# Filler matmuls between the last expert and the output: ten of 64 columns instead of four of 256

## The chip, the core and the metric

One core of one Trainium2 chip runs the whole kernel as one program. The metric is the device time of that core in microseconds (us). Single instructions are given in us or ns. The engines are called PE (TensorE, matrix multiply; PEld is its weight load), DVE (VectorE), ACT (ScalarE), POOL (GpSimd) and SP (SyncE, which here only issues DMAs).

## What is computed

A gated recurrence over 5056 tokens of 4 sequences, 256 channels, is followed by a soft mixture of experts. All tokens are mixed into 32 slots (a softmax over tokens), each of 8 experts transforms its own 4 slots, and each token of the output is a softmax-weighted mixture of the 32 slot outputs:

```python
for t in range(S):                      # S = 5056
    h = f[:, t] * h + i[:, t] * x[:, t]
    y[:, t] = h
# y is then reshaped to 20224 tokens of 256 and called x
logits = x @ phi                        # 20224 x 32
slot_input = softmax(logits, axis=0).T @ x
for e in range(E):                      # E = 8, w1: 256 x 1024, w2: 1024 x 256
    h = np.maximum(slot_input[e] @ w1[e], 0.0)
    slot_out[e] = h @ w2[e]
return softmax(logits, axis=1) @ slot_out.reshape(32, 256)   # 20224 x 256, float32
```

## The kernel before, in words

The kernel has three stages. **The recurrence stage** (lines 452 to 579, about the first 131 us) loads x and f_logit in groups, applies the gates, turns the data to channels on PE, scans along time on DVE, turns it back, and builds the exponentials of the logits, `etall`, and the 32 slot inputs. All instructions stand in an order written out by hand (`manual_schedule`, line 151), so every engine works through its own list in the order of the code.

**The expert stage** (lines 583 to 686, about 131 to 145.5 us) is short and runs on PE almost alone. The second half of the experts is accumulated into two PSUM tiles `so_ps`, one for each half of the 256 output columns (lines 661 to 668). Then DVE scales the first half and ACT the second half into the SBUF tile `slot_out` (lines 683 and 684), and POOL makes from it the two masked copies `slot_bd` (line 686).

**The output stage** (lines 689 to 795) multiplies `etall` with `slot_out` (`share`, line 704) or with `slot_bd` (`couple`, line 753) on PE into the PSUM tiles `op`, scales the rows with `rrow` on DVE (lines 694 and 758) and ACT (lines 698 and 764) into SBUF, and sends the rows out by DMAs that SP issues (lines 730, 741, 767 and 784). The order is that of lines 787 to 795: first block 0 of sequence 0 in small pieces (`pieces`), so that the first DMAs can go out early, then larger parts.

What the change touches is the helper `spin` (lines 143 to 146). It multiplies a piece of the first expert's weights with itself into the PSUM tile `tail`, whose values nobody reads: it is filler, and keeps PE occupied where PE would otherwise wait. Each of its matmuls loads 128 columns of weights and then streams `w` columns. It is called in four places between the slots and the output, in two of them with 21 matmuls of 64 columns, in one with 7 of 256 columns (`SPINS`), and at line 682, after the last expert matmul and before the first output matmul, with 4 of 256 columns (`D` is 256, `P` is 128).

The order around the change is this: on PE the last `so_ps` matmul, the filler of line 682, the first output matmul of line 704; on DVE and ACT the `slot_out` halves, then the first evictions of `op`. The PSUM of the output tiles `op` is the memory that `tail` and the other PSUM tiles leave behind (`held.close()`, line 689), so the first output matmul waits for three things: the DVE half of `slot_out`, the ACT half, and the end of PE's own filler.

Of the kernel before, what the change touches and what calls it, by code (L numbers as in the profile page):

```python
# [18 lines left out]
def kernel(  # L19
# [11 lines left out]
    B, S, D = x.shape  # L31
# [4 lines left out]
    P = 128  # L36
# [106 lines left out]
    def spin(dst, k, w):  # L143
        for _ in range(k):
            nc.tensor.matmul(dst[:, ds(0, w)], w1_sb[0][:, 0, :P], w1_sb[0][:, 0, :w],  # L145
                             start=True, stop=True, skip_group_check=True)
# [9 lines left out]
    with tc.tile_pool(name="sp2", bufs=3) as sp2, \  # L156
# [314 lines left out]
        for n in range(n_unit):  # L471
# [14 lines left out]
            else:  # L486
# [40 lines left out]
                if n == n_unit - 2:  # L527
                    tail = psp.tile([P, 2, G], F32, name="tail", tag="sp")
# [61 lines left out]
    with tc.tile_pool(name="ew", bufs=1) as ew, \  # L590
# [70 lines left out]
        for j in range(Q):  # L661
# [13 lines left out]
            if j == 1:  # L675
# [3 lines left out]
                spin(tail[:, 1], SPINS, D)  # L679
                nc.vector.reciprocal(rrow[:, wide_r:q], rs_ps[:, wide_r:q])  # L680
                nc.vector.reciprocal(rrow[:, q, ds(0, B // 2)], rs_ps[:, q, ds(0, B // 2)])
        spin(tail[:, 1], 4, D)
        nc.vector.tensor_scalar_mul(slot_out[:, ds(0, C)], so_ps[0], rcs)
        nc.scalar.activation(slot_out[:, ds(C, C)], so_ps[1], ACT.Copy, scale=rcs)
        for u in range(2):
# [140 lines left out]
```

## Time and profile before

| | |
|---|---|
| median of 4 runs | 200.76 us (200.65 to 200.94) |
| the profiled execution's own time | 200.85 us |
| its span, first to last instruction | 199.1 us |
| mean granted TensorE clock | 0.861 |
| PE / PEld / DVE / ACT / POOL busy | 152.9 / 110.1 / 143.4 / 138.6 / 103.0 us |
| HBM read, written | 58.23 MB, 20.71 MB |

The profile is one execution; its span is 1.75 us shorter than its time. Times of single instructions are counted from the start of the span. "Granted clock" is the share of its full clock that PE was given. "Busy" of PE is not PE at its peak, since matmuls overlap and their ends are modelled. A releaser is the instruction whose end the profile sees as the last thing that an instruction waited for.

### The profile page before, as it was taken

The page shows a single profiled execution, that of the slowest core. Times are in us where ns is not written, and L with a number is a line of the kernel's source. Part 1 is how long each engine was busy: PE and PEld are TensorE (multiplying, and loading weights), DVE is VectorE, ACT ScalarE, POOL GpSimd, SP SyncE. Part 2 cuts the span into 40 slices and gives each one's busy share as a digit, 9 for nine tenths or more (in the row PEclk, how much of TensorE's full clock was granted, in tenths as well). Part 3 has the DMA queues.
Part 4 walks back from the last instruction along what each step waited for, and adds up shares of the span by engine and source line. Part 5 has one row for each costly group of instructions (what it writes and reads, how often), then busy time and mean ns, then how long its engine had stood idle before and what let it go on. Part 6 is the DMA issues. An engine that isn't in the chain of part 4 may idle for free.

```text
span 199.1 us, 3497 instructions
## 1 busy us (share of the span) xinstructions
PE 152.9 (77%) x1330; PEld 110.1 (55%) x1330; DVE 143.4 (72%) x164; ACT 138.6 (70%) x195; POOL 103.0 (52%) x78
## 2 busy tenths in 40 slices
PE   0588598898979989899897987989989999950000
PEld 0367467676757767668585765567963543310000
DVE  1669879999787999999989999614268878740000
ACT  3689678799688998999987595623069889980000
POOL 2489587884986789774969969390030000000000
PEclk9999979999987999999999999999996555555555
DMA  5999999999999999999999999999429999999995
GB/s 180 414 421 421 433 421 421 433 428 343 391 425 423 426 323 418 426 413 321 397 421 391 220 213 212 211 218 207 79 90 426 419 441 421 421 454 438 421 421 214
DMA packets 14449, 70.77 MB, mean 355 GB/s; under 512 B 1745, under 2 KB 3025, under 8 KB 10465
## 3 DMA queue, kind: packets, MB, share of 16 engines
q1 hardware_dynamic: 11664, 62.13, 75.4%
q0 software_dynamic: 2624, 8.42, 21.2%
q8 instruction: 10, 0.16, 0.3%
q14 instruction: 7, 0.05, 0.1%
q10 hardware_dynamic: 144, 0.00, 0.0%
HBM read 58.23 MB, written 20.71 MB: 397 GB/s over the span
## 4 chain that ended last, share of the span: by engine, by line
PE 41%; DVE 24%; DMA 8%; ACT 8%; issue 4%; POOL 4%; SPq 0%; ACTq 0%; DVEq 0%; POOLq 0%
DVE h L304 17%; PE op L753 12%; DMA f_t<-in_f_logit_dram 8%; PE hp L317 4%; POOL u_t L237 4%; PE up L258 4%; PE sp L252 4%; DVE ht L334 4%; ACT s_t L226 3%; PE op L704 2%; PE slot_ps L174 2%; PE so_ps L664 2%; PE lg L348 2%; ACT a L293 2%; PE tail L145 1%
## 5 line engine op out<-in xcount | busy, mean ns | idle before, releaser
L237 POOL TENSOR_TENSOR u_t<-s_t,x_t 128x1024 bf16<-128x1024 bf16 (+1 forms) x39 | 82.6, 2130 | 24.4 <-ACT s_t L226 11.3
L304 DVE TENSOR_TENSOR_SCAN h<-a,h,up 128x512 bf16<-128x512 f32 (+1 forms) x72 | 86.9, 1252 | 5.5 <-PE up L258 3.8
L226 ACT ACTIVATE s_t<-f_t 128x2048 bf16<-128x2048 f32 (+2 forms) x23 | 38.3, 1670 | 6.4 <-DMA f_t<-in_f_logit_dram 6.3
L317 PE MATMUL hp<-ident_f,h 128*128 128x128 f32 (+1 forms) x160 | 29.6, 310 | 8.3 <-DVE ht L334 5.5
L317 PEld LDWEIGHTS hp<-ident_f,h 128*128 128x128 f32 (+1 forms) x160 | 23.2, 208 | 16.4 <-DVE ht L334 9.7
L252 PE MATMUL sp<-ident_f,s_t 128*128 128x128 f32 x144 | 22.0, 298 | 9.7 <-ACT s_t L226 7.7
L286 ACT ACTIVATE a<-sp,nomlb 128x1024 f32<-128x1024 bf16 x24 | 25.4, 1113 | 1.6 <-PE sp L252 1.0
L753 PE MATMUL op<-slot_bd,etall 64*128 64x512 bf16 x62 | 24.3, 592 | 0.3
L252 PEld LDWEIGHTS sp<-ident_f,s_t 128*128 128x128 f32 x144 | 17.9, 154 | 11.4 <-issue 5.9
L764 ACT ACTIVATE oc<-op,rrow 128x256 f32<-128x256 f32 x60 | 22.8, 490 | 1.4 <-PE op L753 0.9
L758 DVE TENSOR_TENSOR oc<-op,rrow 128x1024 f32<-128x1024 f32 x16 | 19.2, 1222 | 4.7 <-PE op L753 4.6
L293 ACT ACTIVATE a<-sp,nomlb 128x512 f32<-128x512 bf16 (+2 forms) x22 | 17.9, 859 | 4.3 <-PE sp L252 3.9
L258 PE MATMUL up<-ident_f,u_t 64*128 64x64 f32 x192 | 18.2, 233 | 2.6 <-POOL u_t L237 2.5
L258 PEld LDWEIGHTS up<-ident_f,u_t 64*128 64x128 f32 x192 | 14.3, 141 | 6.6 <-POOL u_t L237 3.2
L174 PE MATMUL slot_ps<-rep,ident 128*128 128x256 bf16 x122 | 17.6, 280 | 0.0
L753 PEld LDWEIGHTS <-etall 64*128 64x128 bf16 x62 | 9.0, 152 | 14.2 <-issue 11.8
L334 ACT COPY ht<-hp 128x512 f32<-128x512 f32 (+1 forms) x18 | 10.5, 582 | 8.3 <-PE hp L317 8.3
L334 DVE COPY ht<-hp 128x512 f32<-128x512 f32 (+1 forms) x22 | 14.7, 668 | 1.1 <-PE hp L317 1.1
L174 PEld LDWEIGHTS <-ident 128*128 128x128 bf16 x126 | 11.3, 101 | 3.1 <-issue 1.1
L304 DVE TENSOR_TENSOR_SCAN h<-a,up 128x512 bf16<-128x512 f32 x8 | 9.4, 1212 | 2.7 <-ACT a L293 1.9
L252 PE MATMUL up<-ident_f,u_t 128*128 128x128 f32 x48 | 9.7, 334 | 0.8 <-POOL u_t L237 0.8
L348 PE MATMUL lg<-h,phi 128*32 128x512 bf16 (+1 forms) x80 | 10.1, 412 | 0.0
(105 smaller groups left out, 147.2 us busy)
## 6 DMA issues: line engine op xcount, KB each, us to landing
f_t<-in_f_logit_dram SPq DMA_DIRECT2D x12, 1024.0 KB, 12.7
x_t<-in_x_dram SPq DMA_DIRECT2D x12, 1024.0 KB, 11.5
out_dram<-oc SPq DMA_DIRECT2D x6, 2048.0 KB, 13.4
w_sb<-in_moe_w_dram POOLq DMA_DIRECT2D x14, 512.0 KB, 9.5
f_t<-in_f_logit_dram SPq DMA_DIRECT2D x12, 512.0 KB, 8.7
x_t<-in_x_dram SPq DMA_DIRECT2D x12, 512.0 KB, 8.6
out_dram<-oc SPq DMA_DIRECT2D x4, 896.0 KB, 6.0
out_dram<-ob SPq DMA_DIRECT2D x1, 2048.0 KB, 9.1
```

What stands on the lines that cost most here:

```text
L174: nc.tensor.matmul(slot_bank[:, 1, ds(0, rhs.shape[1])], ident, rhs, start=first and i < 2, stop=False, skip_group_check=True)
L226: nc.scalar.activation(s_t, f_t, ACT.Sigmoid, scale=-1.0)
L237: nc.gpsimd.tensor_tensor(uts[n][:, :r], s_t[:, :r], x_t[:, :r], ALU.mult)
L252: nc.tensor.transpose(ps[:, :, r], t[:, r], ident_f)
L258: nc.tensor.transpose(v[:, :, r], t(r)[k].bitcast(F32), ident_f[k, k])
L286: nc.scalar.activation(a, sp[:, :, :, :, o], ACT.Identity, scale=nomlb[:, ds(o, 1)], bias=1.0)
L293: nc.scalar.activation(decays[n // 2, o][:, ds(n % 2, k), :T], sp[:, ds(n % 2, k), :T, o], ACT.Identity, scale=nomlb[:, ds(o, 1)], bias=1.0)
L304: nc.vector.tensor_tensor_scan(h[:, :T, o], decays[n // 2, o][:, n % 2, :T], up[:, :T, o], hs[number(g - 1, b)][:, ds(used(g - 1) - 1, 1), ...
L317: nc.tensor.transpose(hp[:n_p, r], hw[:, :n_p, r], ident_f)
L334: copy(hts[g][:n_p, b].rearrange("p r d -> p (r d)").bitcast(F32), hps.pop(n)[:n_p].rearrange("p r c -> p (r c)"))
L753: nc.tensor.matmul(op[:, i_r].rearrange("p u d -> p (u d)"), ew[:, :, r + i_r], slot_bd[ds(j * 2 * NS, 2 * NS)].rearrange("s u d -> s (u d)"),
L764: nc.scalar.activation(ob[:, u, r + i_r], op[:, i_r, u], ACT.Copy, scale=scale[:, r + i_r, ds(u, 1)])
```

## The change

One line changes. The filler between the last expert and the output becomes ten matmuls of 64 columns instead of four of 256. Each of them comes with its own weight load, as before; nothing else is moved.

```diff
                 nc.vector.reciprocal(rrow[:, wide_r:q], rs_ps[:, wide_r:q])
                 nc.vector.reciprocal(rrow[:, q, ds(0, B // 2)], rs_ps[:, q, ds(0, B // 2)])
-        spin(tail[:, 1], 4, D)
+        spin(tail[:, 1], 10, P // 2)
         nc.vector.tensor_scalar_mul(slot_out[:, ds(0, C)], so_ps[0], rcs)
         nc.scalar.activation(slot_out[:, ds(C, C)], so_ps[1], ACT.Copy, scale=rcs)
```

## Prediction

> **What bounds the kernel now.** I read the page's slices first, to see which stage the change stands in and what limits the stage after it.
>
> ```profile
> PEclk9999979999987999999999999999996555555555
> DMA  5999999999999999999999999999429999999995
> GB/s 180 414 421 421 433 421 421 433 428 343 391 425 423 426 323 418 426 413 321 397 421 391 220 213 212 211 218 207 79 90 426 419 441 421 421 454 438 421 421 214
> ```
>
> A slice is 4.98 us. The DMA engines are full everywhere but in slices 29 and 30 (139.4 to 149.3 us): that is the expert stage and the first microseconds of the output. From 149 us the output's writes run at about 420 GB/s to the end; 20.4 MB at 0.42 MB/us is 48.5 us, which ends at 197.5. So the end is set by when the output's DMAs get going, and then by their rate. What PE does after 149 us costs nothing unless the DMAs run dry. PE's clock falls to one half in slice 31.
>
> Next, the chain of waits, cut to the change. Columns: start, duration, what.
>
> ```profile
> 145.09 0.45 PE tail L145 x4
> 145.54 0.05 issue
> 145.58 0.45 PE op L704 x2
> 146.03 0.01 issue
> 146.04 0.44 DVE ob L694
> ```
>
> The filler (tail L145) is on this chain, ahead of the first output product and the first eviction. Whether it really holds them is told by the timeline around it (start, duration, instruction, idle time before it and its releaser):
>
> ```profile
> 144.92 0.60 PE L145 MATMUL tail<-w_sb 128*128 128x256 bf16 x4
> 145.07 0.35 DVE L683 TENSOR_SCALAR slot_out<-so_ps,rcs 128x128 bf16<-128x128 f32 x1 [0.97 <-PE so_ps L664]
> 145.12 0.37 ACT L684 ACTIVATE slot_out<-so_ps,rcs 128x128 bf16<-128x128 f32 x1 [7.37 <-PE so_ps L664]
> 145.58 0.43 PE L704 MATMUL op<-slot_out,etall 32*128 32x256 bf16 x2
> 146.04 0.42 DVE L694 TENSOR_TENSOR ob<-op,rrow 128x256 f32<-128x256 f32 x1 [0.62 <-PE op L704]
> 146.53 0.35 SPq L730 DMA_DIRECT2D out_dram<-ob  x1
> ```
>
> The filler ends at 144.92 + 0.60 = 145.52, ACT's half of slot_out at 145.12 + 0.37 = 145.49. Both must be over before the first product, so today the filler is the last by 0.03 to 0.04 us. The product's first result is there at 145.91 (the record of the first of the two lasts 0.32 us from 145.58). DVE starts its eviction only at 146.04. The trace has DVE's own semaphore waits for line 694, which are not counted as busy: six of 0.05 us each, at 145.08, 145.18, 145.28, 145.37, 145.84 and 145.94. The last ends at 145.99, so DVE could not have evicted before about 146.0 had the product been there earlier. Why DVE paused from 145.42 to 145.84 no view tells; the semaphores named in those waits had all been raised by 143.95, and none is PE's. The first DMA, at 146.53, follows DVE's eviction.
>
> [...] half-clock stretches begin at 24.30, 58.44 and 150.60 us, all whole multiples of 3.413 us apart, the first two are 3.41 us long, and the third lasts to the end. [...] The earlier filler of the same shape as the new one settles which:
>
> ```profile
> 132.01 0.78 PE L145 MATMUL tail<-w_sb 128*128 128x64 bf16 x21
> ```
>
> The last of them lasts 0.193 us, so the 20 steps take 0.59 us: 29 ns each[...]. [...] The trace has 98 ns for one, but they follow each other every 29 ns, so they overlap and don't set the pace.
>
> **The change part by part.** Removed: four matmuls of 256 columns. Their pace is (0.60 - 0.27) / 3 = 0.109 us (0.27 is the duration of one), so the group runs from 144.92 to 145.52. Added: ten of 64 columns, 9 x 0.029 + 0.193 = 0.45 us, from 144.92 to 145.37, with the weight loads hidden beside them. The filler ends 0.15 us earlier. It is then no longer the last: ACT's half of slot_out at 145.49 is. The first product can start by 0.03 to 0.04 us earlier, about 145.54, and its result is there at 145.87 instead of 145.91. On DVE nothing moves, since its waits end at 145.99 anyway, and so neither does the first DMA. ACT's first eviction, at 146.10, waits for the second product, and moves by the same 0.04 us; its DMA is issued at 146.93, after SP has spent 0.35 us on DVE's, although its data were ready at 146.59. That 0.04 us lies beside SP's issue. The third product waits for DVE's eviction (146.51 after 146.46). So from 146.0 on everything stands where it stood. Twelve more instructions on PE are fetched while older work runs; I cost them at nothing, and at their pace they would be in the 0.15 us saved. If DVE's pause is not there in other executions, the cover is gone, and the 0.04 us reach the end.
>
> Sum against the profiled execution: 200.85 - 0.00 to 0.04. That execution is 0.09 us over the median of 200.76, within the runs' spread of 0.29 us. I take the middle: 200.76 - 0.02 = **200.74 us**.
>
> There is a second effect, on the clock. [...] I made a measure and tried it on the trace: for each 3.413 us window, the columns streamed by matmuls that start in it, times the share of the 128 x 128 array they use (a float32 transpose counts twice, as four take 0.48 us)[...]. The three windows that end in a drop have 0.28, 0.32 and 0.31; of those at full clock that don't, the lowest has 0.375 (126.70 to 130.12). So the line lies between 0.32 and 0.375. The filler falls into the window 143.77 to 147.18: 20 so_ps matmuls of 128 columns, 4 x 256 of filler, 9 products of 256 columns on a quarter of the array: 2560 + 1024 + 576 = 4160, or 0.51. After: 640 in place of 1024, 3776 or 0.46. Still well over, so the drop comes where it came, at 150.60.
>
> ```profile
> 143.77:147.18 3.41, 2.85 (x37) 2.42 (x35) 1.35 (x5) 0.88 (x3) 1.52 (x2) 1.00 0.02 7
> 147.18:150.60 3.42, 3.16 (x18) 1.86 (x17) 3.29 (x5) 3.42 (x10) 0.31 (x1) 1.00 0.76 282
> 150.60:154.01 3.41, 3.41 (x9) 0.97 (x8) 2.83 (x3) 3.04 (x9) 0.00 (x0) 0.50 1.06 425
> ```
>
> These are the window's length, busy time of PE, PEld, DVE, ACT and POOL, the clock, DMA share and GB/s. The reader is to see that busy time alone doesn't mark the window that ends in the drop (3.16 of 3.42 us busy, yet half clock after it): its products use a quarter or half of the array.
>
> **The rivals.** *The early product passes through (faster).* DVE's pause shrinks with the filler, or is an accident of this execution. Then DVE starts 0.02 us after the result, at 145.89 instead of 146.04, and the first DMA comes 0.15 us earlier at most: 200.76 - 0.15 = 200.61. For it: the chain names PE as releaser. Against it: DVE's recorded waits.
>
> *The clock falls a window earlier (slower).* [...] in another execution they lie differently against the kernel. Sliding my measure over the trace, with the line at 0.35, the last window that holds starts up to 144.48 before and up to 144.24 after. In 0.24 of 3.41 us of positions, 7%, the drop would come 3.4 us sooner, about 147.7; if the true line lay over 0.46, it would in this position too, at 147.18. Price: at half clock a 256-column product takes 0.222 us (16 in 3.56 on the chain) instead of 0.109, a 512-column one 0.43 instead of 0.33. With 7 and 8 of them between 147.18 and 150.60 that is 0.8 + 0.8 = 1.6 us at most. DVE and ACT, 3.29 and 3.42 us busy there, already set the pace, and the DMAs issued by then hide more. Lower bound 0; I take 0.45: 201.2 us.
>
> *The narrow filler is slower than I think (slower).* If behind the expert matmuls the pace were the 98 ns of a weight load, ten would last 9 x 0.098 + 0.193 = 1.08 us, to 146.00. The first product would start 0.48 us late, its result come at 146.39 and DVE start at 146.41, 0.37 us late: 201.13 us. It costs the product something from a pace of 45 ns (the filler then ends at today's 145.52), and DVE from about 54 ns (145.60, by which the 0.08 us ahead of 145.99 are used up). Against it: 41 measured steps of 29 ns.
>
> **How the numbers follow.** Nothing reaches the end: 0.66, at 200.74. Early product passes: 0.16. Clock: 0.10. Slow filler: 0.08. A measurement of this kernel can tell about 0.2%, 0.4 us, from no change. The first two cases lie within it but for 0.06 that I leave to a gain I have not seen; of the last two about 0.10 lies above 201.16. So faster 0.06, same 0.84, slower 0.10. The range, 200.50 to 201.10, takes in the runs' spread under the early product, and most of the slow side.
>
> **What would show it.** In the profile after: ten filler matmuls 29 ns apart, over by 145.4 on this scale; the first product released by ACT's slot_out, about 0.04 us sooner after the last so_ps matmul; DVE's first eviction no earlier than 0.95 us after that matmul's end (145.09); the fall of the clock in the window after the one with the filler. Wrong would be: a filler pace over 45 ns, half clock before the pieces are done, or a first DMA that moves by over 0.15 us.

## The result and the profile after

The kernel with ten narrow fillers takes 200.57 us (median of 35 runs, 200.08 to 201.90), the kernel before 200.62 us in the same set (56 runs, 200.18 to 202.88). The ratio is 0.9996, with a 95% interval of 0.9984 to 1.0009: no difference that can be told. The forecast was 200.74 us and, with a chance of 0.84, no difference that can be told; the range was 200.50 to 201.10.

The profiled execution after took 200.55 us with a span of 198.8 us. The page's slices, in the order of before's:

```profile
PEclk9999999996999999999999999999995555555555
DMA  5999999999999999999999999999529999999995
GB/s 186 414 420 420 429 432 422 425 427 340 398 430 420 399 340 422 432 407 307 412 415 378 241 214 213 213 214 210 87 98 423 424 433 422 429 458 429 422 422 214
```

The output stage looks as before: the DMAs fill up in slice 31 (423 GB/s) and stay full. The place of the change in its chain of waits (start, duration, what):

```profile
144.07 0.40 PE so_ps L664 x4
144.47 0.02 issue
144.50 0.38 ACT slot_out L684
144.87 0.07 issue
144.94 0.42 PE op L704 x2
145.36 0.04 issue
145.40 0.43 DVE ob L694
```

The filler has left the chain. ACT's half of slot_out stands where it stood. The timeline of the same stretch:

```profile
144.29 0.46 PE L145 MATMUL tail<-w_sb 128*128 128x64 bf16 x10
144.44 0.35 DVE L683 TENSOR_SCALAR slot_out<-so_ps,rcs 128x128 bf16<-128x128 f32 x1 [1.80 <-PE so_ps L664]
144.50 0.37 ACT L684 ACTIVATE slot_out<-so_ps,rcs 128x128 bf16<-128x128 f32 x1 [8.20 <-PE so_ps L664]
144.94 0.41 PE L704 MATMUL op<-slot_out,etall 32*128 32x256 bf16 x2 [0.19 <-ACT slot_out L684]
145.40 0.42 DVE L694 TENSOR_TENSOR ob<-op,rrow 128x256 f32<-128x256 f32 x1 [0.61 <-PE op L704]
145.90 5.26 SPq L730 DMA_DIRECT2D out_dram<-ob  x8
```

This stage stands 0.63 us earlier than in before, because the work ahead of it came through earlier, which the change doesn't touch; in a second execution of the same kernel (below) it stands 0.78 us later than here. So I count from the start of DVE's slot_out (line 683) in each trace and call it T; times as "T + 0.96" come from the trace's single records. The filler ends at T + 0.31 instead of T + 0.455. The first product starts at T + 0.499 instead of T + 0.515, and its result is there at T + 0.797 instead of T + 0.839, 0.042 us sooner. DVE's last semaphore wait starts at T + 0.869 (before: 0.874), its eviction at T + 0.963 (0.969), the first DMA's issue at T + 1.458 (1.465). The gain is gone one step after it arises.

What differs between the two profiled executions lies later. In the timeline of SP's queue the second DMA's issue, a single instruction, took 0.98 us in before and 1.29 us in after:

```profile
146.93 0.98 SPq L730 DMA_DIRECT2D out_dram<-ob  x1
```

```profile
146.30 1.29 SPq L730 DMA_DIRECT2D out_dram<-ob  x1
```

And half clock (a granted clock of 0.50) began at T + 5.53 in before, at T + 3.83 in after, in both right after the window that follows the one with the filler. The last byte landed at T + 52.75 and T + 53.05. The 0.30 us in favour of before match the 0.31 us of SP's second issue, which by itself doesn't show that one causes the other. Whether these two things, the held issue and the clock, belong to the change or to the single execution is what most experiments below are about.

### The profile page after: what moved, and what is told of

It is laid out like the page before. It is cut to its first block, busy times and chain, and to the rows that moved or that the text cites. A ratio compares the mean times of both kernels' runs of the same rounds, so it can differ in the third digit from the quotient of the medians.

```text
span 198.8 us, 3509 instructions
## 1 busy us (share of the span) xinstructions
PE 151.1 (76%) x1336; PEld 108.2 (54%) x1336; DVE 143.5 (72%) x164; ACT 138.8 (70%) x195; POOL 103.2 (52%) x78
## 4 chain that ended last, share of the span: by engine, by line
DMA 36%; PE 28%; DVE 15%; POOL 4%; issue 3%; ACT 2%; ACTq 0%; SPq 0%; POOLq 0%
DMA x_t<-in_x_dram 14%; PE op L753 11%; DVE h L304 11%; DMA w_t<-in_moe_w_dram 8%; DMA f_t<-in_f_logit_dram 7%; DMA w_sb<-in_moe_w_dram 7%; PE hp L317 4%; PE up L258 3%; POOL u_t L237 3%; DVE ht L334 3%; PE sp L252 3%; PE op L704 2%; PE slot_ps L174 2%; ACT oc L764 1%; PE lg L348 1%
## 5 line engine op out<-in xcount | busy, mean ns | idle before, releaser
L252 PE MATMUL sp<-ident_f,s_t 128*128 128x128 f32 x144 | 21.2, 290 | 10.3 <-ACT s_t L226 7.8
L252 PEld LDWEIGHTS sp<-ident_f,s_t 128*128 128x128 f32 x144 | 17.4, 150 | 12.0 <-issue 5.9
L258 PE MATMUL up<-ident_f,u_t 64*128 64x64 f32 x192 | 17.6, 229 | 3.1 <-POOL u_t L237 3.1
L252 PE MATMUL up<-ident_f,u_t 128*128 128x128 f32 x48 | 8.9, 314 | 0.8 <-POOL u_t L237 0.8
```

Of the source, the lines that this page charges most:

```text
L252: nc.tensor.transpose(ps[:, :, r], t[:, r], ident_f)
L258: nc.tensor.transpose(v[:, :, r], t(r)[k].bitcast(F32), ident_f[k, k])
```

## Experiments

Every experiment starts from the kernel after. Ratios are against the kernel before on the same chip.

**No filler.** Edit:

```diff
-        spin(tail[:, 1], 10, P // 2)
```

> No filler at all between the last expert matmul and the first output product. If the filler is off the path (my theory), the first product starts as in the kernel after, about 0.50 us after DVE's slot_out begins, since ACT's half of slot_out is the last thing it needs; DVE's first eviction stays at 0.96 us and the first DMA at 1.46 us; time within 0.2% of before. If the early product passes through, and the pause of DVE follows the filler, the eviction comes at about 0.83 us or sooner and the time drops by 0.1 us or more. If the filler is what holds the clock, the window that covers it loses 640 of its columns, about 0.08 of my load measure, so half clock may begin one window (3.41 us) earlier; that rival expects some 0.45 us more.

Measured: ratio 0.9998 (0.9979 to 1.0016). First product at T + 0.47, its result at T + 0.739, DVE's eviction at T + 0.968, first DMA at T + 1.462. The result came 0.10 us sooner than in before and DVE didn't move: its cover holds. That the product came sooner than in the kernel after (start 0.025 us, result 0.058 us) was not expected. The trace has the difference: with a filler, PE's sequencer runs one more semaphore wait ahead of the product's weight load (T + 0.392 to 0.443 in after), since the load then waits for the filler too (the filler is what ended the load's last 0.28 us of idle time in after's timeline; here it was DVE's slot_out, after 0.56 us). It begins at T + 0.468 in after and at T + 0.403 here. In the profiled execution half clock began at T + 1.60, the pieces' products ran slower (the 14 from the third on took 3.03 us instead of 1.90, and the last ended at T + 4.47 instead of 3.34), and the first couple's DMA was issued at T + 8.51 instead of 6.65. The execution took 201.22 us, the longest of the 14 of this kernel, whose median is 199.80. Whether the clock made it long is tested below; on the whole the filler's absence has no cost that can be told.

**Twelve wide fillers.** Edit:

```diff
-        spin(tail[:, 1], 10, P // 2)
+        spin(tail[:, 1], 12, D)
```

> Twelve fillers of 256 columns at the place of the ten of 64. At 0.109 us each and 0.27 for the last the group lasts 1.47 us, 0.87 us more than the four of before. My theory (filler hidden only while it ends ahead of ACT's slot_out and DVE's pause): the product comes 0.87 us later than before, DVE's eviction 0.87 - 0.08 = 0.79 us later, the first DMA too, and the whole output stage with it: about 0.8 us more than before, 0.4%. If instead the start of the output stage has slack (its DMAs run at their rate whatever the first pieces do), the time stays within 0.2%.

Measured: ratio 1.0014 (1.0001 to 1.0027), +0.28 us, a third of what I expected. The timeline has the delay as worked out: filler of 1.47 us, DVE's eviction at T + 1.75, first DMA at T + 2.25, 0.78 us later than before.

```profile
144.71 1.47 PE L145 MATMUL tail<-w_sb 128*128 128x256 bf16 x12
146.24 0.44 PE L704 MATMUL op<-slot_out,etall 32*128 32x256 bf16 x2
146.61 0.42 DVE L694 TENSOR_TENSOR ob<-op,rrow 128x256 f32<-128x256 f32 x1 [1.40 <-PE op L704]
147.10 0.82 SPq L730 DMA_DIRECT2D out_dram<-ob  x2
```

The last line is two DMA issues in 0.82 us; the second took 0.42 us, not 0.98. It was over at T + 3.07, 0.22 us after before's 2.85. The last byte landed 0.35 us later. Here the end goes with the second issue, not the first.

**Forty narrow fillers.** Edit: `spin(tail[:, 1], 40, P // 2)`.

> Forty fillers of 64 columns. At 29 ns a step they last 39 x 0.029 + 0.193 = 1.32 us, 0.72 us longer than the four wide ones of before: product 0.72 us later, DVE and the first DMA 0.64 us later, time 0.6 us more. If the rival of slow narrow fillers is right and each takes the 98 ns of its weight load, they last 4.0 us and the time rises by 3.3 us.

Measured: ratio 1.0067 (1.0046 to 1.0087), +1.3 us. The pace is 29 ns (40 in 1.33 us), so the rival of slow narrow fillers is out:

```profile
143.77 1.33 PE L145 MATMUL tail<-w_sb 128*128 128x64 bf16 x40
```

But its first DMA came 0.14 us sooner than with twelve wide ones, and still it landed 0.8 us later (T + 53.91 against 53.10). Its table of DMA queues has 11 instruction packets on PE's queue, that of twelve wide ones has 10; the eleventh, 16 KB in one packet of 0.88 us, runs at T + 30.95, while the output's DMAs are full.

**More instructions at the very end.** Edit:

```diff
                 if i or j:
                     couple(i, j)
+        op = pout.tile([P, R, D], F32, name="op", tag="op")
+        for _ in range(32):
+            nc.tensor.matmul(op[:, 0, ds(0, P // 2)], ident, ident[:, ds(0, P // 2)],
+                             start=True, stop=True, skip_group_check=True)
```

> The kernel after, with 32 more matmuls of 64 columns (64 instructions with their weight loads) on PE after the very last output product, where PE has nothing more to do and only the output's DMAs still run. Nothing waits for them. The kernel with forty fillers was 1.0 us slower than the kernel with twelve wide ones although its first DMA came sooner; its trace shows one more instruction fetch of PE, 16 KB in one packet of 0.88 us, in the middle of the output's DMAs. If that fetch is the cause, this kernel shows it too and takes about 0.8 us more than the kernel after; if the cause lay in the fillers' place, it takes the same time.

Measured: ratio 1.0072 (1.0046 to 1.0097), +1.4 us, although nothing waits for these matmuls and PE is done with them more than 19 us before the last byte lands. The queue tables of after and of this kernel (kind, packets, MB, share of the DMA engines' time):

```profile
q8 instruction: 10, 0.16, 0.3%
```

```profile
q8 instruction: 11, 0.18, 0.3%
```

With 64 instructions more on PE, q8 has one packet more: it is this queue that I call PE's. The one thing on record that these matmuls bring into the output is the fetch. The second execution of the kernel without filler (below) is a twin of this one until then: SP's second issue is over at T + 2.28 and the first couple's DMA is issued at T + 7.57 in both. The twin's last byte landed at T + 52.71, this kernel's at T + 54.03: 1.3 us later, with the one fetch more. I had expected 0.8 us. One view shows where it arises. The last 23 us of output in both kernels, cut into 40 slices of 0.575 us, up to where the last byte lands; first after, then this kernel:

```profile
GB/s 456 427 456 456 456 456 456 456 456 456 456 456 456 427 399 370 342 313 427 456 456 456 456 456 456 456 456 456 456 456 456 427 427 370 342 370 342 456 29 0
```

```profile
GB/s 456 456 456 427 456 456 456 456 456 427 456 456 399 399 313 427 313 399 456 456 456 456 456 456 456 456 456 456 456 456 456 399 370 370 370 313 57 29 28 0
```

After the DMA engines as a whole are finished, one goes on alone at some 28 GB/s, one sixteenth of 456: about one slice in after, three here. Of the last DMA's 16 landings, 15 come by T + 52.46 in after and one at 53.05; here 14 by 52.26, then 52.87 and 54.03. It looks as if an engine that was already late got the fetch's 0.88 us on top; which engine carried it, the record doesn't say.

**Every piece's product twice.** Edit:

```diff
-                        share(ops[j][:, ds(at[j], k)], i, b, r, k)
+                        for _ in range(2):
+                            share(ops[j][:, ds(at[j], k)], i, b, r, k)
```

> Every product of the first small pieces is done twice on PE (the second overwrites the first with the same values; nothing else changes), which gives these pieces the PE rate of half clock. It prices the rival of an early fall of the clock: it adds 16 products of 0.109 us, 1.74 us of PE work at full clock. The clock rival as I priced it expects 0.45 us more at the end, its upper bound 1.6 us. My own reading, that DVE and ACT set the pace in the pieces and that issued DMAs cover what is left, expects the first product's end and so the first DMA only some 0.1 to 0.25 us later and the end 0.1 to 0.3 us later.

Measured: ratio 1.0072 (1.0047 to 1.0097), +1.4 us: near the 1.6 us that I had as upper bound (too low, as the next section says), and not the 0.1 to 0.3 us that I expected. The first DMA is issued at T + 1.56, only 0.1 us late; the loss is later. Stages (window, its length, busy time of PE, PEld, DVE, ACT, POOL, clock, DMA share, GB/s):

```profile
150.00:152.00 2.00, 1.90 (x7) 0.58 (x4) 1.52 (x2) 1.53 (x5) 0.00 (x0) 0.50 1.03 405
152.00:154.00 2.00, 1.91 (x6) 0.81 (x6) 1.69 (x3) 1.63 (x6) 0.00 (x0) 0.50 0.51 207
152.50:153.25 0.75, 0.75 (x3) 0.35 (x3) 0.75 (x2) 0.38 (x2) 0.00 (x0) 0.50 0.00 0
```

The pieces' 2 MB have gone out by 152.5, and the first couple's DMA, which goes out whole, is not there yet: it is issued at T + 9.05, which is 152.62, and its first bytes move only after 153.25. From 152.5 to 153.25 the DMAs stand still.

**The kernel after, and the one without filler, once more.** No edit.

> The kernel after once more, one look, for another position of the clock windows. The product and DVE's first eviction must stand at 0.50 and 0.96 us after slot_out begins, as before. Where half clock begins is the open part: by my load measure the last window that holds starts no later than about 0.8 us before slot_out begins, so half clock begins between 2.6 - 3.4 and 2.6 + 3.4 us, earliest about -0.4 and never later than 6.1 us after. The later it is, the earlier the first couple's DMA is issued: 6.65 at 5.53 (before), 7.29 at 3.83 (after), 8.51 at 1.60 (no filler).

> The kernel without filler once more, one look. In the first look half clock began 1.60 us after slot_out, the first couple's DMA was issued at 8.51 and the last byte landed at 53.66. If that lateness is the clock's, a look with a later fall issues the couple sooner (about 7 at a fall of 4 or later) and lands near 53.0; if it is the missing filler's, the couple stays at 8.5.

Measured: without filler, half clock now began at T + 3.25, the couple was issued at T + 7.57 and the last byte landed at T + 52.71, against 1.60, 8.51 and 53.66 in the first execution, which ran on another chip. SP's second issue took 0.42 us in both. So one kernel lands 0.95 us apart, and what sets the two traces apart is when the clock falls and what follows from it. Of the 0.95 us, 0.79 are idle time of the DMA engines between T + 6 and T + 12, around the couple's issue. The stage from 152 to 154 us, first execution, then second:

```profile
152.00:154.00 2.00, 1.81 (x6) 0.66 (x5) 2.00 (x2) 1.63 (x6) 0.00 (x0) 0.50 0.44 175
```

```profile
152.00:154.00 2.00, 1.97 (x6) 0.81 (x6) 1.69 (x3) 1.63 (x5) 0.00 (x0) 0.50 0.83 331
```

The kernel after: result at T + 0.796, eviction at T + 0.960, first DMA at T + 1.455, all within 3 ns of the first execution. Half clock began at T + 6.01. SP's second issue took 0.42 us instead of 1.29:

```profile
147.08 0.42 SPq L730 DMA_DIRECT2D out_dram<-ob  x1
```

It was over at T + 2.28 instead of 3.15, and the last byte landed at T + 52.32 instead of 53.05: 0.73 us for 0.87 us of issue. The clock fell later too (6.01 against 3.83), but the pieces' evictions ended at T + 4.73 in both, so the loss doesn't come by way of PE. In the first 6 us from T the DMA engines were busy 0.48 of the time in the first execution and 0.60 in the second (the number next to last in these lines), a difference of 0.72 us; in the 6 us after that both were full.

```profile
144.44:150.44 6.00, 5.15 (x36) 3.21 (x33) 4.16 (x7) 4.37 (x12) 1.84 (x2) 0.82 0.48 175
```

```profile
145.22:151.22 6.00, 5.01 (x36) 3.16 (x33) 4.79 (x7) 4.77 (x13) 1.83 (x2) 1.00 0.60 227
```

So the hold comes and goes between executions of one kernel. What it coincides with is PE's instruction fetch of 16 KB. In the six traces where the fetch ended between T + 2.4 and 3.0 (before, after, the pieces twice, ACT first, and two below) SP's second issue ended at T + 2.85 to 3.35, five times 0.38 to 0.43 us after the fetch; in the other, with fillers where PE waits, the second issue began only after the fetch and took 0.47. Where the fetch was over by T + 1.7 and SP issued the second DMA as here, it took 0.42 or 0.43 us. The other queue that carries instructions (q14) fetches at T + 1.4 to 1.6 in every trace, held or not, so it alone doesn't make the difference.

**ACT first.** Edit:

```diff
-                    for j, by in enumerate((by_vector, by_scalar)):
+                    for j, by in enumerate((by_scalar, by_vector)):
```

> The first of each pair of small pieces is evicted by ACT and the second by DVE (in before and after it is the other way round). ACT has no pause of 0.41 us in its semaphore waits, so the first product is no longer hidden. My theory of the cover expects ACT's first eviction about 0.83 to 0.87 us after DVE's slot_out begins and the first DMA at about 1.35, 0.11 us sooner than the kernel after. Whether that reaches the end: the second DMA's issue, by the traces so far, ends 0.4 us after PE's 16 KB instruction fetch when the fetch falls on it, so if it does again nothing is gained; if it doesn't, at most 0.1 us. The rival that the early product passes through expects 0.1 to 0.15 us less.

Measured: ratio 1.0000 (0.9985 to 1.0016). ACT evicts at T + 0.84, so the sooner product is used, and the first DMA is issued at T + 1.38, 0.08 us sooner than in after. The fetch fell on the second issue (over at T + 3.10 against 3.15), the last byte landed at T + 53.03 against 53.05. With DVE's cover taken away, nothing came through in this execution. Whether the 0.08 us come through where no fetch holds the second issue stays untested: the ratio can't tell less than 0.3 us.

**Fillers where PE waits.** Edit (`hold` multiplies `ident` with a view of `rep`, 256 columns a time):

```diff
+        def hold(dst, k):
+            for _ in range(k):
+                nc.tensor.matmul(dst, ident, rep.rearrange("p b s -> p (b s)").bitcast(BF16),
+                                 start=True, stop=True, skip_group_check=True)
...
                         r, at[j] = r + k, at[j] + k
+                    if r == 2:
+                        hold(ops[0][:, 3], 5)
```

> The kernel after, with five more fillers of 256 columns between the second and the third output product, where PE waits 0.5 us for DVE's eviction. They don't delay the third product (five last 0.109 x 5 + 0.16 = 0.7 us after 0.75, to about 1.45, where it starts now), but add 1280 columns, 0.16 of my load measure, to every clock window that covers them. By that measure the last window that holds full clock then starts up to 1 to 1.5 us later, so half clock begins 2.2 us or more after slot_out in nearly every position of the windows. If an early fall of the clock costs time (0.6 to 0.9 us in the execution of the kernel without filler in which it came at 1.60), the mean falls by 0.1 to 0.3 us. If the clock costs nothing: no change.

Measured: ratio 1.0011 (0.9999 to 1.0023). The experiment didn't isolate the clock. The fillers write into a free column of the PSUM tile that DVE evicts, and DVE then waited for the last of them:

```profile
145.22 0.72 PE L716 MATMUL op<-rep,ident 128*128 128x256 bf16 x5
146.03 0.42 DVE L694 TENSOR_TENSOR ob<-op,rrow 128x256 f32<-128x256 f32 x1 [1.30 <-PE op L716]
```

It evicted at T + 1.65 and the first DMA was issued at T + 2.15. The first DMA is 0.69 us later than in after, SP's second issue was over at T + 3.02, and the last byte landed at T + 53.10.

**The same, and one filler ahead of each pair in the couples.** Edit in addition:

```diff
                 op = pout.tile([P, 2, 2, D], F32, name="op", tag="op")
+                if i == len(blocks) - 1:
+                    hold(op[:, 0, 0], 1)
```

> The kernel with five fillers between second and third output product, and one more filler of 256 columns ahead of each pair of products in the two couples that follow the pieces (8 fillers). At full clock a pair of products takes PE 0.43 us of the 0.72 us that the evictions need, so one more of 0.11 us is hidden; my load measure rises from about 0.31 to 0.45 there, so full clock should hold to about 155 us, past all the pieces and both couples. If the clock's early fall costs time, the couples' DMAs are issued by 1 us or more earlier and the time falls by 0.2 to 0.5 us against before; if not, no change. If the fillers themselves get in the way, half clock plus filler makes PE the bound and the time rises.

Measured: ratio 1.0175 (1.0151 to 1.0199), +3.5 us. This is the last of the three cases that I had set out: half clock began at T + 5.07, when two of the couples' eight fillers had run, and the other six then made PE the bound.

```profile
150.00:152.00 2.00, 2.00 (x6) 0.52 (x5) 0.70 (x2) 1.57 (x4) 0.00 (x0) 0.50 1.03 412
```

**A second queue for ACT's pieces.** Edit (POOL; in the other kernel `nc.scalar` in place of `nc.gpsimd`):

```diff
-                        nc.sync.dma_start(out=dst[:, ds(q, k)], in_=obs[j][:, ds(q, k)])
+                        queue = (nc.sync, nc.gpsimd)[j]
+                        queue.dma_start(out=dst[:, ds(q, k)], in_=obs[j][:, ds(q, k)])
```

> In the small pieces the DMAs of what ACT evicts are issued by POOL instead of SP; the others stay on SP. The traces so far say that SP's second DMA issue, when PE's instruction fetch overlaps it, ends 0.39 us after the fetch (2.42 to 2.96 us after slot_out began, in six kernels), and that the end follows that issue. If the hold is SP's own, SP now goes on to the next DVE piece, whose issue can begin at about 2.6, and POOL, free from slot_bd at 2.43, adds its own: the DMAs are full 0.5 us earlier and the time falls by up to 0.3 us, unless the couples' DMAs, bound by PE's clock, then come too late. If the hold is the DMA engines' own (the fetch sits ahead in them), or the couples bind, nothing is gained. POOL's way of issuing may be slower: then the time rises.

> As the kernel in which POOL issues, but ACT itself issues the DMAs of what it evicts. Same question on SP's hold. Against it: ACT sets the pace of the pieces (3.42 of 3.42 us busy in before), and an issue that costs it about 0.35 us each, as on SP, would slow the pieces by up to 1.4 us and delay the couples; then the time rises by 0.3 to 1 us.

Measured: POOL 0.9989 (0.9971 to 1.0008), no difference; ACT 1.0063 (1.0043 to 1.0084), slower by 1.3 us, somewhat more than expected. In both profiled executions the fetch was over before SP's issues, so they don't answer whether the hold is SP's alone. ACT's issues of 0.34 us stand between its evictions as expected:

```profile
149.40 0.34 ACTq L731 DMA_DIRECT2D out_dram<-ob  x1
149.78 1.21 ACT L698 ACTIVATE ob<-op,rrow 128x256 f32<-128x256 f32 x3 [0.41 <-PE op L704]
151.01 0.34 ACTq L731 DMA_DIRECT2D out_dram<-ob  x1
```

## Why the prediction was right, and where its reasons were not

**The gain and its cover: right, and shown.** The pace of 29 ns (each matmul's weight load takes 98 ns in after, and the loads overlap), the filler's end, ACT as the new releaser, 0.04 us on the product's result (measured 0.042; its start moved by 0.016) and 0 on DVE came as worked out. One thing on PE was left out: the extra semaphore wait that the filler brings, with which goes the 0.06 us by which the result came sooner still without filler. DVE stayed at T + 0.96 there too, so "the early product passes through" is out for this kernel: DVE's eviction stands at 0.960 to 0.970 in before, after and without filler, in both executions where there are two. With DVE's cover removed the first DMA did come 0.08 us sooner, while the end stayed; SP's second issue was held in that execution too. DVE's pause of 0.41 us is in all fourteen traces (its fifth wait starts at T + 0.77 in each), so it was no accident; what makes it stays open.

**"The end is set by when the output's DMAs get going": right in kind, too coarse.** Twelve wide fillers moved the first DMA by 0.78 us and the end by 0.28. Two later things stand between: when SP's second issue is over, and when the first couple's DMA is ready. Whichever leaves the DMAs empty sets the end. The idle time of the 16 DMA engines (a mean over them, counted from T) bears this out: the last byte lands at 49.2 to 49.5 us plus that idle time in all fourteen traces. The second of these two things is where PE counts again, and I had written that PE after 149 us costs nothing unless the DMAs run dry: they did where half clock came early and where the products were doubled.

**The clock.** In before and in both executions of after, the window with the filler held: 0.51, 0.64 and 0.37 on my load measure (my 0.46 was for the narrow filler in before's position of the windows). But in two other kernels with the same ten fillers, ACT first and more instructions at the end, that window, with 0.27 and 0.30, was itself the last at full clock, which ended at T + 2.50 and 2.85. By my measure it thus depends on where the windows fall. Four wide fillers would have added 0.05 there, which leaves both below the lowest window that holds (0.35), so by my measure these two falls are not the change's. The measure, extended to all fourteen, has 36 full-clock windows that end in a drop: 32 with 0.37 or less, four at 0.41, while the lowest that hold have 0.35 and 0.37. The 14 that end full clock for good have 0.31 at most. It sorts well but has no sharp line. The measure is mine, and so is its scale (4160 columns are 0.51 on it); that the clock goes by it is not shown. The windows rest on the clock records: within before the starts of half clock are whole multiples of 3.413 us apart, in after likewise (45.87 and 148.27), and each stretch of half clock that ends again, two in before and one in after, lasted 3.413 us. They lie differently against the kernel from trace to trace: in the fourteen, half clock begins for good anywhere from T + 1.60 to T + 6.81. In the kernel after, half clock began once at T + 3.83 and once at 6.01. The first is behind the pieces' last product on PE (3.34) but ahead of their last eviction (4.73): in part the sign of being wrong that I had named, "half clock before the pieces are done", though from T + 6 on the DMAs were as full as in before (428 and 425 GB/s in the next 6 us).

The **price** in this rival was mis-sized. I took 0.45 us and argued that issued DMAs hide more; measured are 0.95 us between two executions without filler, 1.65 us apart in the fall, and 1.4 us with the pieces' products doubled. What failed is the step "the DMAs issued by then hide more": the pieces are 2 MB, gone by 152.5 us in that last kernel, and the next DMA waits for a whole couple. That DVE and ACT set the pace failed with it, since at half clock the pieces' products ended 1.1 us later. The upper bound was too low as well: I took 0.33 us for a product of 512 columns at full clock, but where PE doesn't wait they start 0.215 us apart in before (149.13 to 149.99). Eight of them then lose 1.7 us instead of 0.8, and the bound is 2.5 us. The rival itself did not come about by the change, in keeping with its chance of a tenth: no run shows the narrow filler shifting the fall's odds, and the ratio leaves 0.1% for it at most.

**"Twelve more instructions, I cost them at nothing": right for twelve, wrong as a rule.** Sixty-four more cost 1.4 us where nothing waited for them. The traces show fetches by a DMA queue of their own, q8, in packets of 16384 bytes: ten in before and ten in after, each while PE was at work, and each 0.88 to 0.97 us long but for after's last with 1.20. That they are fetched while older work runs held; that this costs nothing did not hold as a rule: a fetch took 0.88 us of one of 16 full DMA engines, or went with an issue that took up to 0.96 us longer (1.38 us with the pieces twice, in place of 0.42). Kernels with 2737 recorded PE instructions or fewer had ten such fetches, those with 2765 and more eleven; the change went from 2693 to 2705.

**The size.** 200.74 forecast, 200.57 measured, with before at 200.62 in the larger set instead of 200.76 in the four runs shown. The runs spread wider than those four told: the two chances of each execution, where the clock falls and whether the fetch meets SP's second issue, are worth up to 0.95 and 0.73 us, some twenty times the 0.04 us of the change. They aren't the whole of the spread. The stages ahead of the change vary as well: T itself stands at 144.44 and 145.23 us in the two executions of the kernel after, and these two times, 200.55 and 200.59, agree only because the later start met the quicker output. That the profile after is 0.30 us shorter than the one before is of the same kind, and nothing to do with the change. No kernel tried is faster than before and after by more than the noise.

## What to carry to other kernels

Follow a saved wait one step further than its own releaser: here ACT's slot_out, DVE's own semaphore waits, SP's issues and the size of the next DMA each stood in the way of 0.04 us. In a stage that runs at the DMAs' rate, ask when the DMAs would be empty, and look at the instruction fetches too: here 64 added instructions that nothing waits for cost 1.4 us. A difference between two profiled executions is first to be tested against a second profile of the same kernel.

## What the runs showed of the hardware that was not expected

- One DMA engine seems to finish alone, at 28 to 29 GB/s of 456 in after and in the kernel with more instructions at the end: in twelve of the fourteen traces the last of the final DMA's 16 landings is 0.46 us or more behind the one before it (0.6 us in before and after), and in the two kernels where a fetch of 16 KB fell among full DMAs that tail was 0.94 and 1.16 us.
- In five traces a DMA issue on SP that met PE's 16 KB fetch ended about 0.4 us after the fetch did, and took 0.8 to 1.4 us in place of 0.42. Why, and whether other engines' issues are held too, is not shown.
- DVE stops for 0.41 us after four semaphore waits behind slot_out, in all fourteen traces, with the semaphores named in these and the next wait long raised (by 1.1 us ahead of T in before, 0.4 us in after); ACT's first six waits at the same place start 0.08 us apart in before and after, without such a pause.
